# Plain second layer in the first two later groups, with the weights' sums made two groups later

## The chip, the cores and the metric

The kernel runs on one core of one Trainium2 chip. The time is that of the device in microseconds (us); 676.91 us is the median of three runs of the kernel before. A profile of one execution, 673.3 us long, gives the busy times and waits of the engines: TensorE (PE in the profile, its weight loads PEld), VectorE (DVE), ScalarE (ACT), GpSimd (POOL) and the DMA queues, of which SyncE (SP) issues nearly all.

## The reference

A recurrent attention block (a decaying state per head) feeds a two-layer block with a gate. All inputs are float32.

```python
# attention, for each time t, batch b, head h (4 batches, 8 heads, 768 steps, 64 wide)
state = gamma * state + outer(k[t], v[t])
y[t] = scale * q[t] @ state
x = y as (3072 tokens, 512)

# two-layer block: w_in (512, 2048), w_out (2048, 512)
h = x @ w_in
g = h * erf(softplus(h))
out = g @ w_out
```

## The kernel before

**Groups.** The 2048 hidden features are split, and so are the tokens. Groups 0 to 3 are the first 512 tokens with 512 features each, computed plainly. From group G0 = 4 up to 23 come the later groups, to which the change belongs: 256 tokens (a "chunk") and 1024 features each, so two groups, `s = 0` and `s = 1`, make a chunk, and both add into the same outputs. Group 4 and 5 are the first chunk of these, 6 and 7 the second.

**First layer of a later group.** `hidden_steps` (L951) computes 26 products of sums in place of 32 plain ones: 26 steps of two matmuls 128x128x128. A float32 matmul leaves two records in the trace, so a step is four records. Each step's product goes to one of four PSUM tiles (banks 0 and 1 are called `hp`, 2 and 3 `r`), and is added to or subtracted from blocks of `h`: the first write of a block is a copy on ScalarE (L974, L976), each later one an addition on VectorE (L972). A step that writes a tile waits for the reads of what was in it. Step 5 is the first with an update on VectorE; steps 1, 5, 9, 13, 15, 16, 19 and 23 to 25 use bank 0. The weights of the steps are sums of blocks of `w_in`, made in place once (`W_SUMS`, `sum_in`, L344): those of `s = 0` on VectorE during group 4, of `s = 1` twenty on GpSimd and ten on VectorE.

**The gate.** `gate_softplus` and `gate_erf` run on ScalarE over 128x2048 values, and `gated` (L854) multiplies on VectorE; the result is `E[g]`, in the buffer `e` (or `r` for groups 1 and 3).

**Second layer of a later group.** `project_part` (L1015) makes seven products of four matmuls with 256 columns (eight records), in place of eight in a plain one: `PRODUCTS` pairs sums of gated values (`S1` to `S4`, made by `g_sums`, L1009, four additions) with sums of weights (`T1` to `T4`). The latter are made once for each `s` by `sums` (L354), each an operation of 128x1024 on VectorE; `last_steps` hands them out one by one. `put_part` (L1041) adds the products up into outputs on VectorE. The plain second layer of groups 0 to 3 is `project` (L890), with 512 columns, whose matmuls are at L901, and `put_first` copies out.

**The order** is written by hand. The loop over `g` issues group g's steps; between steps `order` says after which step n a piece of other work is issued: the next chunk's scalings and transposes (`prepared`: L542, L551 twice, L555 twice), `g_sums`, `last_steps`. After steps 14, 18 and 24 comes a product of group g - 1, and after the loop the attention of a later chunk (`sub_visit`, L718) and group g - 1's other products. Each engine works its own queue in the order of issue, so an operation on VectorE holds up all that is issued behind it.

The sums of `w_out` for `s = 0` are issued at the end of group 4 (two) and after steps 1 and 3 of group 5 (two, ahead of step 5's update). Those for `s = 1` are issued after step 22 of group 5, after steps 12 and 22 of group 6, and at the end of group 6. The last plain steps of group 3, `project(3, 0)` and `project(3, 1)`, stand ahead of group 4's loop, the two others behind it:

```python
    project(G0 - 1, 0)
    x_sums(G0)
    sub_begin(j)
    project(G0 - 1, 1)
    sub_states(j)
    sum_in(0, 20)
```

`x_sums` (L942) makes the sums of inputs on VectorE. `sub_begin` makes scores into two tiles `r` on TensorE, and `sub_states` reads these on VectorE (L640, L666).

Of the kernel before, what the change touches and what calls it, by code (L numbers as in the profile page):

```python
# [12 lines left out]
F32 = mybir.dt.float32  # L13
# [6 lines left out]
P = 128  # L20
C = 128
TCH = 512
FG = 4
SCH = 256
# [112 lines left out]
def kernel(  # L137
# [13 lines left out]
    nc = tc.nc  # L151
# [10 lines left out]
    DH = d_model // 2  # L162
# [555 lines left out]
    def sub_visit(j, g):  # L718

        c = j % NC
        m, i = divmod(j, JPC)
        if i == 0:
            XC[m] = ret.tile([P, HP, TCH], F32, name="xT")
        pp = [ret_psum() for _ in range(2)]
        clear = set()

        def first(*bank):  # L730
            new = bank not in clear
            clear.add(bank)
            return new

        def of_state(a):
            t = slice(a * D, (a + 1) * D)
            for u in PAIRS:
                for r in range(2):
                    col, own = u // 2, slice(r * D, (r + 1) * D)
                    x = state_1 if g == G0 else state  # L740
                    nc.tensor.matmul(  # L741
                        pp[r][col * D : (col + 1) * D, u % 2, t], x[own, u, :], QT[j][own, u, t],
                        start=first(r, col), stop=True, skip_group_check=True,
                    )

        other = SC[j + 1] = [ret_psum(ps_h) for _ in range(2)]

        def of_values(crossed):  # L750
            for u in PAIRS:
                for a in range(2):
                    r = 1 - a if crossed else a
                    col, t = u // 2, slice(a * D, (a + 1) * D)
                    own = slice(col * D, (col + 1) * D)
                    nc.tensor.matmul(
                        other[a][own, u % 2, D:] if crossed else pp[a][own, u % 2, t],
                        V[j][t, 2 * u + r, :],
                        AM[j][t, r, u, :D],
                        start=crossed or first(r, col), stop=True, skip_group_check=True,  # L760
                    )

        if c:
            of_state(0)
        last = chunk_of(g - 1)
        if (g - G0) % 2 == 1:
            clear.update((("o", 0), ("o", 1)))
        new = [
            None if g == G0 else O[last][3][:, 1, :].rearrange("p (u d) -> p u d", d=D),
            pp[1][:, 2:, :].rearrange("p a (b d) -> p (a b) d", d=D),  # L770
        ]
        adds = range(int(g == G0), 2 if c < NC - 1 else 1)
        for u in range(HP):
            for r in range(2):
                for a in adds:
                    t, h = slice(a * D, (a + 1) * D), 2 * u + r
                    nc.tensor.matmul(  # L777
                        new[a][r * D : (r + 1) * D, u, :], KQ[j][t, 0, h, :], V[j][t, h, :],
                        start=first("o" if a == 0 else 1, r), stop=True, skip_group_check=True,
                    )  # L780
        if g > G0 and c:
            nc.vector.tensor_tensor(state, state, new[0], op=ALU.add)
        elif g > G0:
            nc.vector.tensor_copy(state, new[0])
        of_values(False)
        of_values(True)
        if j + 1 < NJ:
            sub_scores(j + 1)
            sub_mask(j + 1)
        of_state(1)  # L790
        for r in range(2):
            a = 1 - r
            x, y = XC[m][:, r::2, i * C : (i + 1) * C], other[a][:, :2, D:]
            if c or a:
                nc.scalar.copy(x, pp[r][:, :2, :])
                x = x[:, :, a * D : (a + 1) * D]
                nc.vector.tensor_tensor(x, x, y, op=ALU.add)
            else:
                nc.scalar.copy(x[:, :, D:], pp[r][:, :2, D:])
                nc.scalar.copy(x[:, :, :D], y)  # L800
        if c < NC - 1:
            nc.vector.tensor_tensor(state, state_1 if g == G0 else state, new[1], op=ALU.add)
# [14 lines left out]
    def gate_softplus(g):  # L817


        name = "r" if g < 4 and g % 2 else "e"  # L820
        E[g] = act.tile([P, N], F32, name=name, bufs=1)
        nc.scalar.activation(E[g], HS[g], AF.Softplus)  # L822

# [97 lines left out]
    G0 = n_ft // FG  # L921
# [5 lines left out]
    def chunk_of(g):  # L927
        return TCH // SCH + (g - G0) // 2
# [109 lines left out]
    started = set()  # L1038
    R = {}

    def put_part(m, step):  # L1041


        o26, o57, o34, o1 = (O[m][i] for i in range(4))
        if step == 0:
            R[m] = act.tile([P, 8, DH], F32, name="r", bufs=1)
            nc.scalar.copy(R[m][:, 7], o1[:, 0])
            return
        r = R[m]
        t0 = m * SCH  # L1050
        if step == 1:
            nc.vector.tensor_tensor(
                r[:, 0:5:4], o26, r[:, 7:8].to_broadcast([P, 2, DH]), op=ALU.add
            )
        elif step == 2:
            nc.vector.tensor_tensor(
                r[:, 5:7], o57, r[:, 4:5].to_broadcast([P, 2, DH]), op=ALU.add
            )
            nc.vector.tensor_tensor(r[:, 3], r[:, 6], o57[:, 0], op=ALU.add)
        else:  # L1060
            nc.vector.tensor_tensor(r[:, 1:3], r[:, 5:7], o34, op=ALU.add)
            for t in range(2):
                nc.sync.dma_start(
                    out[t0 + t * P : t0 + (t + 1) * P, :],
                    r[:, 2 * t : 2 * t + 2].rearrange("p a c -> p (a c)"),
                )
# [103 lines left out]
    def all_of(steps):  # L1170
        for _ in steps:
            pass
# [10 lines left out]
    project(G0 - 1, 0)  # L1183
    x_sums(G0)
    sub_begin(j)
    project(G0 - 1, 1)
    sub_states(j)
    sum_in(0, 20)

    put = None  # L1190
    for g in range(G0, NG):
        first, even = g == G0, (g - G0) % 2 == 0
        more = j < NJ
        if put is not None:
            put_part(put, 0)
        e_sums = iter(()) if first else g_sums(g - 1)
        next(e_sums, None)
        next_chunk = prepared(j + 1) if even or put is None else iter(())

        if put is not None:  # L1200
            order = {18: (e_sums,), 20: (e_sums,), 24: (e_sums, e_sums)}
        else:
            order = {
                10: (next_chunk,), 14: (next_chunk, e_sums), 16: (next_chunk, e_sums),
                18: (next_chunk, e_sums), 20: (e_sums,), 24: (next_chunk,),
            }
        if g == G0 + 1:
            order.update({1: (last_steps,), 3: (last_steps,), 22: (last_steps,)})
        elif g == G0 + 2:
            order.update({12: (last_steps,), 22: (last_steps,)})  # L1210
        for n, _ in enumerate(hidden_steps(g), start=1):
            if first:
                sum_in(0, min(20 + n, len(W_SUMS)))
                if n == 10:
                    nc.gpsimd.tensor_copy(idle[:, :1], w_in_sb[:, 0, W_SUMS[-1][0], :1])
                    sum_in(1, 20, nc.gpsimd)
            if put is not None and n in (14, 16, 18):
                put_part(put, n // 2 - 6)
            for steps in order.get(n, ()):
                next(steps, None)  # L1220
            if not first and n in (14, 18, 24):
                project_part(g - 1, {14: 1, 18: 2, 24: 4}[n])
        put = None
        all_of(e_sums)
        all_of(next_chunk)

        nc.scalar.activation(idle[:, 1:], idle[:, 1:], AF.Softplus)
        gate_softplus(g)
        if more:
            sub_visit(j, g)  # L1230
        if g + 1 < NG and not even:
            x_sums(g + 1)
        if more:
            if even and not first:
                all_of(prepared(j + 2))
            if j + 3 < NJ:
                load(j + 3)
            j += 1
        gate_erf(g)
        if first:  # L1240
            sum_in(1, len(W_SUMS))
            for tt in range(2, TT):
                project(g - 1, tt)
            put_first()
        else:
            if g == G0 + 2:
                all_of(last_steps)
            for p in (5, 6, 7, 3):
                project_part(g - 1, p)
            if even:  # L1250
                put = chunk_of(g - 1)
        if g == NG - 1:
            last_gated(g)
        else:
            gated(g)
        if first:
            for _ in range(2):
                next(last_steps)

    g, m = NG - 1, chunk_of(NG - 1)  # L1260
    for p, step in ((1, 0), (7, None), (2, None), (6, 1), (5, 2)):
# [56 lines left out]
```

## Time and profile before

| | us |
|---|---|
| time, median of 3 runs (lowest to highest) | 676.91 (675.51 to 677.26) |
| span of the profiled execution | 673.3 |
| TensorE busy | 657.0 |
| weight loads busy | 558.1 |
| VectorE busy | 519.7 |
| ScalarE busy | 272.1 |
| GpSimd busy | 23.0 |

A row of the order of time has the start and the length in us, the engine, the line, the operation, the tile written, the tiles read, shapes and the number of instructions merged into it; a bracket is the time that the engine idled before it, with what ended that. A list of waits has a total, the number of waits and the longest. A row of the windows has for each engine the busy time and the number of instructions, then the granted TensorE clock (1.00 is full), the share of the DMA engines and GB/s. Busy shares are a mean over stages: VectorE is busy 77% of the span, but in the stretch from 160 to 170 us it is busy 9.46 of 10 us and TensorE 5.42.

### The profile page before, as it was taken

What the parts mean: (1) busy time and instruction counts of PE and PEld (TensorE: products, weight loads), DVE (VectorE), ACT (ScalarE), POOL (GpSimd) and SP (SyncE); (2) the same over time, 40 slices, a digit from 0 to 9 for tenths busy, and PEclk for the clock granted to TensorE, in tenths of its full rate; (3) what the DMA queues carried; (4) which work ended last, traced back from release to release, by engine and by line L of the source; (5) the groups of instructions that cost most, each with busy time, mean ns of one, the idle gap of its engine ahead of it and who ended that gap; (6) DMA issues with size and microseconds to landing.
All of it is one profiled execution on the core that took longest, in us unless ns stands there. A gap on an engine that the chain in (4) does not pass through costs nothing.

```text
span 673.3 us, 15344 instructions
## 1 busy us (share of the span) xinstructions
PE 657.0 (98%) x6240; PEld 558.1 (83%) x6240; DVE 519.7 (77%) x1107; ACT 272.1 (40%) x394; POOL 23.0 (3%) x42
## 2 busy tenths in 40 slices
PE   8999999987998999999999999999999999999998
PEld 7744444474997999999999999999999999999997
DVE  5999999988888678677777787787688688476464
ACT  3467453325244243343442442542542542433440
POOL 1000000254000000000000000000000000000000
PEclk9999999999899999999999999999999999999999
DMA  9999953333222222232221231232232220000000
GB/s 187 227 246 217 223 146 87 62 62 59 88 45 45 69 37 46 34 80 45 43 70 33 46 79 35 46 77 38 43 78 40 39 59 1 1 34 1 1 32 32
DMA packets 156726, 47.70 MB, mean 71 GB/s; under 512 B 143088, under 2 KB 147568, under 8 KB 156656
## 3 DMA queue, kind: packets, MB, share of 16 engines
q1 hardware_dynamic: 156240, 46.72, 32.2%
q8 instruction: 49, 0.80, 0.5%
q14 instruction: 21, 0.17, 0.1%
q10 hardware_dynamic: 416, 0.01, 0.0%
HBM read 40.39 MB, written 6.29 MB: 69 GB/s over the span
## 4 chain that ended last, share of the span: by engine, by line
PE 90%; DVE 5%; SPq 2%; DMA 1%; issue 1%; ACT 1%; DVEq 0%; ACTq 0%
PE o L1027 35%; PE hp L960 21%; PE r L960 11%; PE hp L865 8%; PE o L901 7%; SPq L187 2%; PE r L741 1%; PE hp L633 1%; DVE w_in_sb L344 1%; PE o L777 1%; DVE h L972 1%; DVE w_out_sb L354 1%; DMA kq<-in_k_dram 1%; PE r L562 1%; PE o L609 1%
## 5 line engine op out<-in xcount | busy, mean ns | idle before, releaser
L960 PE MATMUL hp<-xs,w_in_sb 128*128 128x128 f32 x1040 | 147.0, 277 | 7.0 <-DVE h L972 6.1
L1027 PE MATMUL o<-w_out_sb,h 128*128 128x256 f32 (+1 forms) x648 | 144.1, 379 | 2.5 <-DVE w_out_sb L354 2.2
L960 PEld LDWEIGHTS hp<-xs,w_in_sb 128*128 128x128 f32 x1040 | 135.7, 193 | 11.3 <-DVE h L972 7.4
L972 DVE TENSOR_TENSOR h<-h,hp 128x256 f32<-128x256 f32 x200 | 81.9, 418 | 75.0 <-PE hp L960 70.2
L1027 PEld LDWEIGHTS o<-w_out_sb,h 128*128 128x128 f32 x648 | 120.5, 190 | 19.6 <-DVE w_out_sb L354 2.6
L1027 PE MATMUL o<-w_out_sb,e 128*128 128x256 f32 x480 | 114.1, 381 | 1.2 <-DVE w_out_sb L354 1.2
L1027 PEld LDWEIGHTS o<-w_out_sb,e 128*128 128x128 f32 x480 | 87.3, 191 | 11.0 <-DVE w_out_sb L354 1.4
L822 ACT ACTIVATE e<-h 128x2048 f32<-128x2048 f32 x22 | 42.0, 1911 | 130.1 <-DVE h L972 130.0
L974 ACT COPY h<-hp 128x256 f32<-128x256 f32 x40 | 14.9, 373 | 154.1 <-PE hp L960 146.0
L972 DVE TENSOR_TENSOR h<-h,r 128x256 f32<-128x256 f32 x160 | 59.9, 415 | 21.6 <-PE r L960 20.5
L960 PE MATMUL r<-xs,w_in_sb 128*128 128x128 f32 x480 | 67.1, 276 | 0.0
L960 PEld LDWEIGHTS r<-xs,w_in_sb 128*128 128x128 f32 x480 | 60.3, 193 | 0.0
L865 PE MATMUL hp<-xT,w_in_sb 128*128 128x512 f32 (+2 forms) x144 | 56.5, 548 | 0.0
L854 DVE TENSOR_TENSOR e<-h,e 128x1024 f32<-128x1024 f32 x42 | 49.3, 1214 | 8.0 <-ACT e L835 8.0
L960 PE MATMUL hp<-xT,w_in_sb 128*128 128x128 f32 x320 | 48.7, 275 | 0.0
L865 PEld LDWEIGHTS hp<-xT,w_in_sb 128*128 128x128 f32 x144 | 25.8, 190 | 27.0 <-issue 24.6
L960 PEld LDWEIGHTS hp<-xT,w_in_sb 128*128 128x128 f32 x320 | 43.7, 192 | 1.9 <-issue 1.0
L835 ACT ACTIVATE e<-e 128x2048 f32<-128x2048 f32 (+1 forms) x23 | 42.1, 1836 | 0.2
L976 ACT ACTIVATE h<-hp 128x256 f32<-128x256 f32 x60 | 23.0, 384 | 35.3 <-PE hp L960 33.9
L960 PE MATMUL r<-xT,w_in_sb 128*128 128x128 f32 x240 | 33.3, 275 | 0.0
L835 ACT ACT_TABLE_LOAD x24 | 30.8, 1283 | 0.4
L960 PEld LDWEIGHTS r<-xT,w_in_sb 128*128 128x128 f32 x240 | 30.0, 192 | 0.0
(156 smaller groups left out, 774.9 us busy)
## 6 DMA issues: line engine op xcount, KB each, us to landing
w_out_sb<-in_moe_w_out_dram SPq DMA_DIRECT2D x14, 512.0 KB, 5.8
kq<-in_k_dram SPq DMA_DIRECT2D x23, 256.0 KB, 4.0
v<-in_v_dram SPq DMA_DIRECT2D x23, 256.0 KB, 3.2
out_dram<-r SPq DMA_DIRECT2D x23, 256.0 KB, 2.7
kq<-in_q_dram SPq DMA_DIRECT2D x288, 16.0 KB, 1.8
kb<-in_k_dram SPq DMA_DIRECT2D x288, 16.0 KB, 1.7
w_in_sb<-in_moe_w_in_dram SPq DMA_DIRECT2D x8, 512.0 KB, 12.1
w_in_sb<-in_moe_w_in_dram SPq DMA_DIRECT2D x8, 256.0 KB, 8.1
```

Source lines behind the costliest of these rows:

```text
L187: nc.sync.dma_start(to[part, u * C : (u + 1) * C].rearrange("p (a d) -> p a d", d=32), src[2 * u + s, :, d * 32 : (d + 1) * 32].rearrange( ...
L344: (engine or nc.vector).tensor_tensor(w_in_sb[:, s, to], w_in_sb[:, s, a], w_in_sb[:, s, b], op=OP[sign])
L822: nc.scalar.activation(E[g], HS[g], AF.Softplus)
L835: nc.scalar.activation(E[g][:, half], E[g][:, half], AF.Erf)
L854: nc.vector.tensor_tensor(E[g][:, half], HS[g][:, half], E[g][:, half], op=ALU.mult)
L865: nc.tensor.matmul(HP_[ft][:, t], w_in_of(ft, kk), XC[0][:, kk, t], start=(kk == 0), stop=(kk == n_k - 1),)
L901: nc.tensor.matmul(O[0][tt].rearrange("p (d c) -> p d c", d=2), E[g][:, u * TCH + tt * P : u * TCH + (tt + 1) * P], w_out_of(ft), start=(f ...
L960: nc.tensor.matmul(to[:, u, :], w_in_sb[:, s, w, u * P : (u + 1) * P], XS[m](x), start=first and u == 0, stop=True, skip_group_check=True,)
L972: nc.vector.tensor_tensor(h, h, of, op=ALU.add if plus else ALU.subtract)
L974: nc.scalar.copy(h, of)
L976: nc.scalar.activation(h, of, AF.Copy, scale=-1.0)
L1027: nc.tensor.matmul(O[m][i][:, half, at], G[g][a][:, u * P : (u + 1) * P], w_out_sb[:, s, OUT[b], u, at], start=i not in started, stop=(s = ...
```

## The change

Groups 4 and 5 compute the second layer plainly (`project_plain`): eight parts, each two matmuls with 512 columns, straight from the gated values and the loaded weights. So no sums are needed for them, and the weights' sums are issued later: `s = 0` in group 6 (after steps 12, 15, 20, 22), `s = 1` in group 7 (14, 16) and group 8 (12, 22). Their outputs are copied on ScalarE (`put_plain`) in group 7. Parts 3 to 7 read `E[g]` after the next gate has begun, so group 5's gate gets the buffer `r`. The attention's addition for the state in group 5, which had used half of a bank begun by a product, now begins its bank itself. Beside this, `project(3, 1)` is issued after step 10 of group 4 in place of ahead of its loop, and the pieces of `prepared` in group 4 come after steps 12, 16, 18, 20 and 22, where they came after 10, 14, 16, 18 and 24.

```diff
-        if (g - G0) % 2 == 1:
+        if (g - G0) % 2 == 1 and g > G0 + 1:
             clear.update((("o", 0), ("o", 1)))
...
-        name = "r" if g < 4 and g % 2 else "e"
+        name = "r" if g < G0 + 2 and g % 2 else "e"
...
+    def project_plain(g, i):
+        m, s = chunk_of(g), (g - G0) % 2
+        t, fh, pair = i // 4, i % 4 // 2, i % 2
+        if m not in O:
+            O[m] = {i: ps_o.tile([P, 2, DH], F32, name=f"o{i}") for i in (0, 1, 3)}
+        for u in range(2 * pair, 2 * pair + 2):
+            at = (2 * fh + t) * TCH + u * P
+            nc.tensor.matmul(
+                O[m][t],
+                E[g][:, at : at + P],
+                w_out_sb[:, s, 2 * fh : 2 * fh + 2, u, :],
+                start=(s == 0 and i % 4 == 0 and u == 0),
+                stop=(s == 1 and i % 4 == 3 and u == 3),
+                skip_group_check=True,
+            )
+
+    def put_plain(m, t):
+        if t == 0:
+            R[m] = act.tile([P, 8, DH], F32, name="r", bufs=1)
+        r = R[m][:, 2 * t : 2 * t + 2].rearrange("p a c -> p (a c)")
+        nc.scalar.copy(r, O[m][t].rearrange("p a c -> p (a c)"))
+        nc.sync.dma_start(out[m * SCH + t * P : m * SCH + (t + 1) * P, :], r)
...
     sub_begin(j)
-    project(G0 - 1, 1)
     sub_states(j)
...
-    put = None
+    plain, put = (G0, G0 + 1), None
...
-        if put is not None:
+        if put is not None and put > chunk_of(G0):
             put_part(put, 0)
-        e_sums = iter(()) if first else g_sums(g - 1)
+        e_sums = iter(()) if g - 1 in plain or first else g_sums(g - 1)
...
-        if g == G0 + 1:
-            order.update({1: (last_steps,), 3: (last_steps,), 22: (last_steps,)})
+        if first:
+            order = {n: (next_chunk,) for n in (12, 16, 18, 20, 22)}
         elif g == G0 + 2:
-            order.update({12: (last_steps,), 22: (last_steps,)})
+            order.update({n: (last_steps,) for n in (12, 15, 20, 22)})
+        elif g == G0 + 3:
+            order.update({n: (last_steps,) for n in (14, 16)})
+        elif g == G0 + 4:
+            order.update({n: (last_steps,) for n in (12, 22)})
...
                 if n == 10:
+                    project(g - 1, 1)
...
             if put is not None and n in (14, 16, 18):
-                put_part(put, n // 2 - 6)
+                if put > chunk_of(G0):
+                    put_part(put, n // 2 - 6)
+                elif n < 18:
+                    put_plain(put, n // 2 - 7)
...
-                project_part(g - 1, {14: 1, 18: 2, 24: 4}[n])
+                part = (14, 18, 24).index(n)
+                if g - 1 in plain:
+                    project_plain(g - 1, part)
+                else:
+                    project_part(g - 1, (1, 2, 4)[part])
...
-            if g == G0 + 2:
-                all_of(last_steps)
-            for p in (5, 6, 7, 3):
-                project_part(g - 1, p)
+            if g - 1 in plain:
+                for part in range(3, 8):
+                    project_plain(g - 1, part)
+            else:
+                for p in (5, 6, 7, 3):
+                    project_part(g - 1, p)
...
-        if first:
-            for _ in range(2):
-                next(last_steps)
```

## The prediction

> **What bounds the kernel now.** I read the page first, then TensorE's waits, then its order of time around each wait, then the clock in short windows, then VectorE's order of time beside it. On the page:
>
> ```profile
> PE 657.0 (98%) x6240; PEld 558.1 (83%) x6240; DVE 519.7 (77%) x1107; ACT 272.1 (40%) x394; POOL 23.0 (3%) x42
> PE   8999999987998999999999999999999999999998
> PEclk9999999999899999999999999999999999999999
> PE 90%; DVE 5%; SPq 2%; DMA 1%; issue 1%; ACT 1%; DVEq 0%; ACTq 0%
> ```
>
> TensorE is busy 98% of the span and carries 90% of the chain that ended last. What can be won without less arithmetic are its 16 us of idling, and the sliced row puts most of them in slices 9, 10 and 13 (one slice is 16.8 us), where the later groups begin. The list of waits, TensorE only, names what it waits for:
>
> ```profile
> PE hp L960 <- DVE h L972: 6.1, 3, 3.9
> PE o L1027 <- DVE w_out_sb L354: 3.4, 2, 2.2
> PE hp L960 <- ACT h L974: 0.7, 1, 0.7
> ```
>
> The order of time on TensorE puts them in groups: the first two lines are group 4 (the first later one), the next four are group 5, the last two are group 6. The bracket is the idle time ahead of the row.
>
> ```profile
> 143.81 0.71 PE L960 MATMUL hp<-xs,w_in_sb 128*128 128x128 f32 x4 [1.74 <-DVE h L972]
> 149.40 0.71 PE L960 MATMUL hp<-xs,w_in_sb 128*128 128x128 f32 x4 [0.51 <-DVE h L972]
> ...
> 161.91 0.68 PE L960 MATMUL hp<-xs,w_in_sb 128*128 128x128 f32 x4 [0.73 <-ACT h L974]
> ...
> 167.79 1.16 PE L960 MATMUL hp<-xs,w_in_sb 128*128 128x128 f32 x8 [3.85 <-DVE h L972]
> 168.78 1.47 PE L960 MATMUL r<-xs,w_in_sb 128*128 128x128 f32 x8
> 170.04 1.91 PE L960 MATMUL hp<-xs,w_in_sb 128*128 128x128 f32 x8
> ...
> 207.77 1.99 PE L1027 MATMUL o<-w_out_sb,e 128*128 128x256 f32 x8 [1.20 <-DVE w_out_sb L354]
> ...
> 218.48 3.72 PE L1027 MATMUL o<-w_out_sb,h 128*128 128x256 f32 x16 [2.15 <-DVE w_out_sb L354]
> ```
>
> After the wait of 3.85 us the same eight records take 1.47 and 1.91 us, where they take 1.06 elsewhere. The windows show why: the granted clock (the column after POOL) is halved.
>
> ```profile
> 168.00:170.00 2.00, 2.00 (x16) 2.00 (x16) 1.52 (x5) 0.39 (x1) 0.00 (x0) 0.82 0.21 33
> 170.00:172.00 2.00, 2.00 (x11) 2.00 (x10) 1.43 (x5) 0.00 (x0) 0.00 (x0) 0.50 0.15 25
> ```
>
> VectorE's order of time says what TensorE waited for: four sums of second-layer weights stand ahead of the updates of h in group 5. In group 4 eight sums of first-layer weights stand ahead of the first update.
>
> ```profile
> 133.78 0.41 DVE L666 COPY state<-r 128x256 f32<-128x256 f32 x1
> 134.11 3.13 DVE L344 TENSOR_TENSOR w_in_sb<-w_in_sb 128x256 f32<-128x256 f32 x8
> 138.16 0.42 DVE L972 TENSOR_TENSOR h<-h,hp 128x256 f32<-128x256 f32 x1 [0.92 <-PE hp L960]
> ...
> 162.53 4.87 DVE L354 TENSOR_TENSOR w_out_sb<-w_out_sb 128x1024 f32<-128x1024 f32 x4
> ```
>
> An undisturbed group is 25.92 us long (222.20 to 248.12 to 274.04 in the chain of waits). Group 5 runs from 159.24 to 191.88, 32.64 us; group 6 to 222.04, 30.16 us. They are 6.72 and 4.24 us too long: this is what the change is aimed at.
>
> [...] 3.85 us of idling was followed by the clock of 0.50, while 1.74 and 2.15 us left it at 1.00. [...] a first-layer sum takes 0.39 us (3.13 for eight) before GpSimd's twenty sums begin at 142.11, and 0.65 us (6.55 for ten, from 153.79) beside them.
>
> **The change, part by part.**
>
> *Second layer plain in groups 4 and 5.* Removed per group: 7 products of 8 records at 0.216 us (eight take 1.73 us in the chain), 12.1 us. Added: 8 parts of 4 records over 512 columns; sixteen such records (L901) take 6.97 us from 152.27 to 159.24, 0.436 each, so 32 take 13.9 us. All of it is on TensorE's path: +1.8 us for each group, +3.7 in all. The three parts inside the loop take 4 x 0.436 = 1.74 us each, as a product does; the excess falls after the loop, five parts for four products. VectorE loses eight sums of gated values (L1009, about 0.6 us each), which it had room for.
>
> *Weight sums taken out of groups 4 to 6.* Group 5 loses its 3.85 us and the slow clock behind it. The slow clock costs 1.9 us: the four pieces after the wait take 1.16, 1.30, 1.71 and 2.15 us in the chain, against 0.89 three times and 1.73. ScalarE's 0.73 us stays, since the copies of the first output still stand ahead of its copies of h. VectorE then reaches group 5's first update after the gating at about 163, when that update's matmuls are just done. Group 5 becomes 25.92 + 0.73 + 1.74 = 28.4 us, for 32.64: -4.2.
>
> *Group 6.* It loses the waits of 1.20 and 2.15 us for sums, since its parts read weights as loaded: 25.92 + 1.74 = 27.7. But four sums of 1.15 us now stand in VectorE's queue at steps 12, 15, 20 and 22. A first-layer step (two matmuls, four records, 0.447 us) writes a PSUM tile whose previous values VectorE must have added to h. Behind the sum at step 12 wait the two updates of steps 13 and 14; step 15 waits for them. Before has the same sum there, and its piece up to step 18 is 3.87 us long against 3.52 in group 7: 0.35. Behind the sum at step 22 and the one at 20 waits the update of step 24, for which step 25 waits: VectorE does them in 4.9 us, and TensorE is there 4.4 us after the part at step 18, so 0.4. Group 6 is 28.4, for 30.16: -1.7.
>
> *Groups 7 and 8.* In 7 two sums take the place of the 2.4 us of output additions (L1052 to L1061), and the output copies go to ScalarE, which idles 4 us there: nothing. In 8 a sum stands at step 12, as in group 6 of before: +0.4. The other, at step 22, is hidden behind the part at step 24.
>
> *Output and buffers.* Group 5's gate moves to the buffer "r", whose last store was issued at about 161, twenty us before: nothing. The state's addition starts its own bank: the same matmuls.
>
> *The plain step inside group 4.* This is the part with a price. The step (8 records, 3.5 us) leaves its place ahead of group 4's loop and stands after step 10. TensorE so begins the loop at 132.2 for 135.8, while VectorE, the slower of the two there, begins its eight sums at 134.11 as before. I carried the rows' durations along both queues. Step 3 needs a tile that L666 reads until 134.19: TensorE waits 1.2 us. Step 9 needs the tile that step 5's update reads; that update is behind the eight sums and ends at 137.65: another 0.8. Steps 9 and 10 end at 138.6 and the moved step at 142.1. VectorE has ended its sums at 140.6 and idles 2.2 us, until step 11 gives it something. From there it is late: four updates, the scaling of keys (0.6 us, 0.9 beside GpSimd) and then step 13's update, for which step 15 waits 1.6 us; step 23 waits 0.4; and step 25 waits 1.7 us for an update that stands behind both transposes, since the second now comes at step 22 and not 24. That sums to 5.7 us of waits and ends the loop at 152.9. The same walk along the old queues gives 3.0 us of waits and 150.3, and the trace has 2.6 and 150.4. So +2.6 us. No single wait reaches the 3.85 us that halved the clock, so I put nothing for it.
>
> *Sum.* +2.6 - 4.2 - 1.7 + 0.4 = -2.9 us, which I take as -3.0; 676.91 becomes 673.9.
>
> **The rivals.**
>
> *A: the moved step fills waits, as it is meant to.* The 1.74 us wait is just where it is put, and if VectorE is not late, group 4 costs nothing: -2.9 - 2.6 = -5.5, 671.4. Against it: VectorE idles only 1.4 us in group 4 before.
>
> *B: the gain is half eaten.* The close waits of group 4 (1.2 and 0.8 us within 5 us) lower the clock as at 168, +1.9: -1.0, 675.9. [...] Against it: 2.6 us of work lie between them.
>
> *C: slower.* In before, three sums cost group 6 most of 4.2 us. If the eight sums in groups 6 to 8 (9.7 us) still hold up TensorE for half their length, 4.9 for the 1.2 us I put (0.75 and 0.4), the sum is -3.0 + 3.7 = +0.7, and with B's clock +2.6: 679.5. Against it: no matmul waits for these sums themselves any more.
>
> **How the numbers follow.** The forecast gets 0.5, A 0.22, B 0.18, C 0.10. The bound of 0.3% is 2.0 us: faster is below 674.9. The forecast is there in 17 cases of 20, A always; B is within, C slower or within. Faster 0.64, same 0.26, slower 0.10. The range, 670.8 to 677.2, reaches past A by the 0.6 us that the two waits put into group 6 and 8 could fall short, and up to B with 1.3 us more, leaving C's worse end out.
>
> **What would show it.** Right: no wait for L354 is left in TensorE's list; group 5 has no wait over 1 us and a clock of 1.00; groups 5 and 6 are about 28.4 us long; group 4's loop shows waits before steps 3, 9, 15 and 25 and ends about 2.6 us later, with VectorE idle near 141 to 143. Wrong: a clock under 1.00 in group 4, or waits over 1 us in groups 6 to 8 for L972.

## The result and the profile after

The changed kernel takes 672.50 us (median of four runs, 672.36 to 672.79) for 676.80 (675.51 to 677.26): a ratio of 0.994, 95% interval 0.9923 to 0.9957. The whole interval lies below the prediction's bound of 0.3% (0.997), so the change is faster. The forecast was 673.9. The profiled executions, 675.38 us before and 672.36 after, have spans of 673.3 and 670.3 us: 3.0 us apart, which is what the forecast took off.

The page of the changed kernel, busy times and slices:

```profile
PE 658.7 (98%) x6192; PEld 547.4 (82%) x6192; DVE 510.6 (76%) x1095; ACT 272.8 (41%) x395; POOL 22.1 (3%) x42
PE   8999999989999999999999999999999999999998
PEclk9999999999999999999999999999999999999999
```

TensorE is busy 1.7 us longer in a span that is 3.0 us shorter. The dents in slices 10 and 13 and the one in the clock are gone; slice 9 keeps one. TensorE's list of waits:

```profile
PE hp L960 <- DVE h L972: 3.8, 5, 1.4
...
PE r L960 <- DVE am L640: 0.8, 1, 0.8
PE hp L960 <- ACT h L974: 0.7, 1, 0.7
```

No wait for L354, a sum of second-layer weights, is left. The longest wait for an update of h is 1.4 us where it was 3.9. There are more of them, and TensorE's order of time says where:

```profile
133.94 1.13 PE L960 MATMUL r<-xs,w_in_sb 128*128 128x128 f32 x8 [0.75 <-DVE am L640]
...
137.57 1.16 PE L960 MATMUL hp<-xs,w_in_sb 128*128 128x128 f32 x8 [0.71 <-DVE h L972]
138.56 3.60 PE L901 MATMUL o<-w_out_sb,r 128*128 128x512 f32 x8
...
145.22 0.71 PE L960 MATMUL hp<-xs,w_in_sb 128*128 128x128 f32 x4 [1.27 <-DVE h L972]
...
149.23 1.16 PE L960 MATMUL hp<-xs,w_in_sb 128*128 128x128 f32 x8 [0.18 <-DVE h L972]
151.75 0.71 PE L960 MATMUL hp<-xs,w_in_sb 128*128 128x128 f32 x4 [1.36 <-DVE h L972]
...
164.26 0.68 PE L960 MATMUL hp<-xs,w_in_sb 128*128 128x128 f32 x4 [0.73 <-ACT h L974]
...
206.78 0.71 PE L960 MATMUL hp<-xs,w_in_sb 128*128 128x128 f32 x4 [0.27 <-DVE h L972]
```

The rows from 133.94 to 151.75 are group 4: TensorE waits before steps 3, 9, 15, 23 and 25, with the moved plain step (L901) at 138.56 between. VectorE's order of time in the same stretch shows the other side:

```profile
139.56 0.87 DVE L344 TENSOR_TENSOR w_in_sb<-w_in_sb 128x256 f32<-128x256 f32 x2
142.72 1.42 DVE L972 TENSOR_TENSOR h<-h,r 128x256 f32<-128x256 f32 x4 [2.28 <-PE r L960]
144.05 0.78 DVE L542 TENSOR_TENSOR kq<-kq,kq_s 128x512 f32<-128x512 f32 x1
```

VectorE, the slower engine of this group, idles 2.28 us while TensorE does the moved step. In the stretch of group 5 where the clock fell before, it now stays at 1.00:

```profile
165.00:170.00 5.00, 5.00 (x39) 4.37 (x38) 3.79 (x10) 1.14 (x3) 0.00 (x0) 1.00 0.24 39
170.00:175.00 5.00, 5.00 (x31) 3.72 (x30) 3.15 (x7) 1.86 (x3) 0.00 (x0) 1.00 0.66 208
```

Read from the starts of the groups on TensorE:

| stretch | before, us | forecast | changed, us |
|---|---|---|---|
| group 5 begins at | 159.24 | +2.6 | 161.58 (+2.3) |
| group 5 | 32.64 | 28.4 | 28.53 |
| group 6 | 30.16 | 28.4 | 28.47 |
| group 7 | 25.92 | 25.9 | 25.92 |
| group 8 | 25.92 | 26.3 | 26.35 |

Summed, the last column against the first is +2.34 - 4.11 - 1.69 + 0.43 = -3.03 us. So what the trace shows is accounted for. Left are the 1.3 us between this and the medians' 4.3, and the question whether each price was rightly understood: the move inside group 4, the plain layer, the clock.

### The profile page after: what moved, and what is told of

Read it like the earlier page. It is cut to its first block, busy times and chain, and to the rows that moved or that the text cites. A ratio compares the mean times of both kernels' runs of the same rounds, so it can differ in the third digit from the quotient of the medians.

```text
span 670.3 us, 15241 instructions
## 1 busy us (share of the span) xinstructions
PE 658.7 (98%) x6192; PEld 547.4 (82%) x6192; DVE 510.6 (76%) x1095; ACT 272.8 (41%) x395; POOL 22.1 (3%) x42
## 4 chain that ended last, share of the span: by engine, by line
PE 77%; DVE 9%; SPq 5%; issue 3%; DMA 3%; ACT 2%; DVEq 0%; ACTq 0%
PE o L1027 33%; PE hp L960 22%; PE r L960 11%; SPq L187 4%; PE o L1048 4%; DMA kq<-in_k_dram 2%; PE r L741 2%; PE hp L633 1%; DVE w_out_sb L317 1%; PE o L901 1%; DVE w_out_sb L325 1%; PE o L777 1%; DVE xs L325 1%; DVE h L972 1%; DVE w_in_sb L331 1%
## 5 line engine op out<-in xcount | busy, mean ns | idle before, releaser
L1027 PE MATMUL o<-w_out_sb,h 128*128 128x256 f32 (+1 forms) x584 | 129.5, 379 | 0.4 <-DVE r L1306 0.4
L1027 PEld LDWEIGHTS o<-w_out_sb,h 128*128 128x128 f32 x584 | 108.6, 190 | 15.4 <-DVE r L1306 0.6
L1027 PE MATMUL o<-w_out_sb,e 128*128 128x256 f32 x432 | 102.2, 379 | 0.0
L822 ACT ACTIVATE e<-h 128x2048 f32<-128x2048 f32 x21 | 40.1, 1911 | 123.0 <-DVE h L972 123.0
L1027 PEld LDWEIGHTS o<-w_out_sb,e 128*128 128x128 f32 x432 | 78.2, 191 | 8.5
L854 DVE TENSOR_TENSOR e<-h,e 128x1024 f32<-128x1024 f32 x40 | 46.9, 1214 | 8.1 <-ACT e L835 8.1
L835 ACT ACTIVATE e<-e 128x2048 f32<-128x2048 f32 (+1 forms) x22 | 40.2, 1833 | 0.2
```

What stands on the lines that cost most here:

```text
L835: nc.scalar.activation(E[g][:, half], E[g][:, half], AF.Erf)
L854: nc.vector.tensor_tensor(E[g][:, half], HS[g][:, half], E[g][:, half], op=ALU.mult)
L1027: nc.tensor.matmul(O[m][i][:, half, at], G[g][a][:, u * P : (u + 1) * P], w_out_sb[:, s, OUT[b], u, at], start=i not in started, stop=(s = ...
```

## The experiments

Theory: a sum or a step costs what it delays in VectorE's queue, and a wait of TensorE like the 3.85 us of before costs a second time through the clock (1.9 us there by the prediction's estimate). Rivals: the plain step in group 4 is a help or neutral; prices simply add; only the plain layer can make room for the sums. The kernel before ran beside them, with medians of 676.98, 676.97 and 676.45 us in the three sets of runs. Its runs at one and the same mean clock, 0.997, have medians of 675.66, 675.44 and 675.48 us, so times of different sets can be laid side by side to within some 0.2 us.

**Group 4's edits undone, in the changed kernel.**

```diff
     sub_begin(j)
+    project(G0 - 1, 1)
     sub_states(j)
...
-            order = {n: (next_chunk,) for n in (12, 16, 18, 20, 22)}
+            order = {n: (next_chunk,) for n in (10, 14, 16, 18, 24)}
...
-                    project(g - 1, 1)
```

> The changed kernel with both edits inside group 4 undone (the plain step of group 3 ahead of the loop again, the pieces of the next chunk after steps 10, 14, 16, 18, 24). Theory of the two queues (VectorE is the slower engine in group 4, so starting TensorE's steps earlier only makes it wait, and the moved step then lets VectorE idle): TensorE's waits in group 4 fall from 4.3 to about 2.6 us, group 5 begins at about 159.2 us in place of 161.6, and nothing after it changes: span 668.0, time 2.3 us under the changed kernel, 670.2. Rival (the plain step fills waits that would be there anyway): the waits of step 15 return beside nothing gained, and the time is 672.5 or more.

Measured: 670.39 us (670.02 to 671.96), ratio 0.9905 (0.9885 to 0.9924), span 668.0. The rows of group 4 are those of before:

```profile
143.82 0.71 PE L960 MATMUL hp<-xs,w_in_sb 128*128 128x128 f32 x4 [1.74 <-DVE h L972]
149.41 0.71 PE L960 MATMUL hp<-xs,w_in_sb 128*128 128x128 f32 x4 [0.51 <-DVE h L972]
```

The edits inside group 4 cost the change 672.50 - 670.39 = 2.1 us of its gain, 2.3 us between the profiled spans.

**One of the two at a time.** First only the step put back ahead of the loop (first and last hunk above), then only the order of the pieces (the middle hunk).

> The changed kernel with only the plain step of group 3 put back ahead of group 4's loop; the pieces of the next chunk stay after steps 12, 16, 18, 20, 22. Theory of the two queues: waits before step 15 (2.0 us), 23 (0.4) and 25 (1.7) remain, the loop ends 1.0 to 1.4 us earlier than in the changed kernel: 671.3. If the place of the step alone were the price, all 2.3 us would come back: 670.2. If the order of the pieces alone were the price, nothing: 672.5.

> The changed kernel with only the pieces of the next chunk put back to steps 10, 14, 16, 18, 24 of group 4; the plain step stays after step 10. Theory of the two queues: the waits before steps 3 and 9 stay (1.5 us together), those before 15 and 25 fall to 0.7 each; the loop ends 1.6 to 1.8 us earlier: 670.8. If the place of the step alone were the price: 672.5.

Measured: 672.02 us (671.72 to 672.08) with the step back, 670.76 (670.60 to 670.88) with the order back. The second is as expected. The first is 0.7 us above its number: the step's place gives 0.5 us back, and the order of the pieces 1.7. With the order back, the waits before steps 15 and 25 are 0.56 and 0.51 us, for 1.27 and 1.36 in the changed kernel. In the run with the step back the clock fell in group 4:

```profile
142.00:146.00 4.00, 1.95 (x16) 1.76 (x15) 3.77 (x8) 0.45 (x2) 3.92 (x6) 0.95 0.23 36
146.00:150.00 4.00, 4.00 (x25) 4.00 (x25) 3.35 (x7) 1.41 (x2) 3.61 (x6) 0.62 0.21 33
```

The wait ahead of it was 2.05 us long. But the one run of five whose mean clock was 1.000 took 671.88 us, hardly less than the 672.03 of the four at 0.997. Here the slow clock seems to take the place of waits for VectorE: before steps 23 and 25 the list has 0.7 us, where 2.1 were expected. So the clock doesn't account for the 0.7 us of the miss; what does was not shown.

**Only group 4's edits, in the kernel before.**

```diff
-    project(G0 - 1, 1)
     sub_states(j)
...
-        if g == G0 + 1:
+        if first:
+            order = {n: (next_chunk,) for n in (12, 16, 18, 20, 22)}
+        elif g == G0 + 1:
...
                 if n == 10:
+                    project(g - 1, 1)
```

> The kernel before with only the two edits inside group 4 (plain step after step 10, pieces after 12, 16, 18, 20, 22); second layer and weight sums as before. Theory of slack: group 4 ends 2.3 us later as in the changed kernel, but VectorE, which holds up group 5, isn't later, because its ten first-layer sums run beside less of GpSimd's work; so group 5's wait falls from 3.9 to about 1.6 us and the clock isn't halved: net +2.3 - 2.3 - 1.9 = -1.9 us, about 675 for 676.8. Rival (the parts add up): +2.3 us, 679.

Measured: 675.84 us (674.08 to 677.77), ratio 0.9979 (0.9970 to 0.9989). The same edits that cost 2.1 us in the changed kernel gain 1.1 here; the prices don't add. Group 5 begins at 161.89, and the longest waits of groups 5 and 6 are

```profile
168.30 1.16 PE L960 MATMUL hp<-xs,w_in_sb 128*128 128x128 f32 x8 [1.72 <-DVE h L972]
...
217.35 5.37 PE L1027 MATMUL o<-w_out_sb,h 128*128 128x256 f32 x16 [2.15 <-DVE w_out_sb L354]
```

1.72 us for 3.85: TensorE came 2.7 us later, VectorE only 0.5 (the wait for its first update of h in group 5 ends at 168.30 for 167.79). In the changed kernel, which has the same edits in group 4, its ten first-layer sums ahead of these updates take 4.40 us for 6.55 in before (GpSimd's own end at 156.53 for 158.40). This is the slack of the theory. The second row shows that group 6's wait of 2.15 us, harmless in the profile of before (3.72 us for the sixteen records after it), here was followed by 5.37 us, with the clock at 0.55 from 217 to 220. Eight of the 22 runs have a mean clock of 1.000 and take 674.08 to 674.42 us; the other 14, at 0.997, have a median of 675.91. The theory's 1.9 us were thus missed by 0.8 at the median, because in most runs the clock fell after all; the one profile, of a run at 0.997, has the fall at group 6's wait, and group 5's windows at 1.00.

**Three sums ahead of group 5's updates, for four**, in the kernel before.

```diff
-            order.update({1: (last_steps,), 3: (last_steps,), 22: (last_steps,)})
+            order.update({1: (last_steps,), 15: (last_steps,), 22: (last_steps,)})
```

> The kernel before with one of the four weight sums that stand ahead of group 5's first update (the fourth, T3 of s = 0) moved to after step 15 of group 5. Theory [...]: group 5's wait falls from 3.9 to about 2.6 us, the clock stays at 1.00, and the time falls by 1.2 + 1.9 = 3.1 us, to 673.7; the runs also spread less. Rival (the clock's loss shrinks with the wait, or isn't bound to it): 1.2 to 1.8 us, 675.3.

Measured: 675.73 us (674.42 to 677.39), 1.2 us less than before: the rival's number. The wait was 2.71 us and the clock fell all the same, for longer than in the profile of before:

```profile
166.00:169.00 3.00, 2.45 (x11) 2.45 (x12) 1.85 (x5) 0.34 (x1) 0.00 (x0) 0.50 0.24 39
169.00:172.00 3.00, 3.00 (x16) 3.00 (x15) 1.92 (x5) 0.05 (x1) 0.00 (x0) 0.50 0.16 26
172.00:175.00 3.00, 3.00 (x19) 2.67 (x18) 2.92 (x5) 0.00 (x0) 0.00 (x0) 0.89 0.84 255
```

That the clock stays at 1.00 after a wait shorter than the 3.85 us of before was an estimate of mine: that part of my theory fell.

**The sums spread, no plain layer**, in the kernel before.

```diff
-            order.update({1: (last_steps,), 3: (last_steps,), 22: (last_steps,)})
+            order.update({12: (last_steps,), 15: (last_steps,), 20: (last_steps, e_sums), 22: (last_steps,)})
         elif g == G0 + 2:
-            order.update({12: (last_steps,), 22: (last_steps,)})
+            order.update({12: (last_steps,), 15: (last_steps,), 20: (last_steps, e_sums), 22: (last_steps,)})
...
-        if first:
-            for _ in range(2):
-                next(last_steps)
```

> The kernel before, second layer by seven products everywhere, with its eight weight sums merely spread: four after steps 12, 15, 20 and 22 of group 5, four after the same steps of group 6, and none ahead of group 5's updates. Group 4 as before. If the deferral is what pays and the plain layer is only a way to it, group 5 is 25.9 + 0.7 + 2.8 = 29.4 us (32.6 before) and group 6 25.9 + 2.8 = 28.7 (30.2 before): span 668.7, time 671.4 or so, about 1 us better than the changed kernel. If VectorE can't carry four sums beside the sums of gated values, each group loses 4 us or more and the time is 674 or above.

Measured: 671.13 us (670.98 to 671.27), groups 5 and 6 29.8 and 28.6 us long. Spreading the sums alone beats the change by 1.4 us; against the changed kernel with group 4 undone it is 0.7 slower. Its groups 5 and 6 are 3.9 and 2.7 us longer than an undisturbed one, the changed kernel's 2.6 each: spread like this, the sums of groups 5 and 6 cost somewhat more than the plain layer with its sums in group 6 (and 0.4 us in group 8).

**The plain step after step 8**, in the changed kernel with the old order of pieces.

```diff
-            order = {n: (next_chunk,) for n in (12, 16, 18, 20, 22)}
+            order = {n: (next_chunk,) for n in (10, 14, 16, 18, 24)}
...
+                if n == 8:
+                    project(g - 1, 1)
                 if n == 10:
-                    project(g - 1, 1)
```

> The changed kernel with the plain step of group 3 after step 8 of group 4 in place of step 10, and the pieces of the next chunk after steps 10, 14, 16, 18, 24. Theory of the two queues: step 9 has to wait for step 5's update anyway, so the plain step fills that wait, the wait of step 3 stays, and the loop ends 0.4 us earlier than with the step ahead of the loop: 669.8, 2.7 us under the changed kernel. Rival (any place inside the loop costs): as with the step after step 10 and these pieces, 670.8.

Measured: 670.83 us (670.50 to 671.10), span 668.8, the rival's number. The step fills the wait before step 9, but the wait before step 3 remains (0.75 us) and that before step 15 is 1.33. My number had left the first out of the sum, though the text names it: -0.4 + 0.75 is near the +0.4 us measured against the step ahead of the loop (670.83 for 670.39). Neither of the two places inside the loop that were tried did better than the one ahead of it.

**Each sum where VectorE idles, no plain layer**, in the kernel with the sums spread.

```diff
         if g == G0 + 1:
-            order.update({12: (last_steps,), 15: (last_steps,), 20: (last_steps, e_sums), 22: (last_steps,)})
+            order.update({5: (last_steps,), 10: (last_steps, next_chunk), 19: (last_steps,), 24: (next_chunk, last_steps)})
         elif g == G0 + 2:
-            order.update({12: (last_steps,), 15: (last_steps,), 20: (last_steps, e_sums), 22: (last_steps,)})
+            order.update({1: (last_steps,), 5: (last_steps,), 14: (last_steps, next_chunk, e_sums), 24: (next_chunk, last_steps)})
```

> As the run with the sums spread over steps 12, 15, 20 and 22, second layer by seven products everywhere and group 4 as before, but each sum is put where VectorE idles anyway: after steps 5, 10, 19 and 24 of group 5 and after 1, 5, 14 and 24 of group 6. Theory (the waits come from what a sum delays behind it, not from VectorE lacking time): group 5 is 25.9 + 0.7 + 0.3 = 27.0 us, group 6 25.9; span 673.3 - 5.7 - 4.2 = 663.4, time 665.6, well under the changed kernel without any plain layer. Rival (VectorE lacks the time for four sums beside the sums of gated values): as the spread one, 671.1.

Measured: 666.42 us (666.29 to 666.65), ratio 0.9856 (0.9844 to 0.9869), span 664.2: the fastest of all, 6.1 us below the changed kernel. The only rows of TensorE in groups 5 and 6 that show a wait are these two:

```profile
161.83 0.68 PE L960 MATMUL hp<-xs,w_in_sb 128*128 128x128 f32 x4 [0.73 <-ACT h L974]
...
168.47 0.71 PE L960 MATMUL hp<-xs,w_in_sb 128*128 128x128 f32 x4 [0.21 <-DVE h L972]
```

VectorE had the time for all eight sums; only their places were wrong. In group 5 it now works with hardly a pause from 162.62 to 178.1 us, and still hardly keeps TensorE waiting. Group 5 is 27.8 us and group 6 26.0. What group 5 has over 25.92 + 0.73 lies ahead of step 15, where TensorE stands for 0.4 us (168.10 to 168.47), and in the attention after step 26: from that step's start to the next product TensorE takes 2.92 us (177.01 to 179.93), in group 6 2.56. The remaining 0.4 us I could not place.

**The same for the changed kernel**, with group 4's edits undone.

```diff
-            order.update({n: (last_steps,) for n in (12, 15, 20, 22)})
+            order.update({1: (last_steps,), 5: (last_steps,), 14: (last_steps, next_chunk), 24: (next_chunk, last_steps)})
...
-            order.update({n: (last_steps,) for n in (12, 22)})
+            order.update({n: (last_steps,) for n in (1, 5)})
```

> The changed kernel with group 4's edits undone and its sums put into VectorE's idle places too: after steps 1, 5, 14 and 24 of group 6, 14 and 16 of group 7, 1 and 5 of group 8. No wait for a displaced update should be left in groups 6 and 8: 0.7 us less than with group 4 undone alone, or 669.4 to 669.7. Beside the run with the same places and no plain layer it gives the plain layer's price alone: 3.7 us by the sum of records (two groups, 13.9 for 12.1 us each); if the plain layer also freed VectorE for something, less.

Measured: 668.91 us (668.71 to 668.97). The sums cost nothing any more in groups 6 and 8: group 8 is 25.92 us again, and group 6 is 215.64 - 188.08 = 27.56 us, so the plain layer costs 27.56 - 25.92 = 1.6 us there. Moving the sums gave 0.9 us in group 6 and 0.4 in group 8, where 0.7 in all was expected. Against the kernel with the same places and no plain layer, the plain layer loses 2.5 us in all; it isn't the full 3.3, since group 5 then holds no sums (28.5 us beside 27.8).

**Only one group's sums moved**, in the kernel before: those of s = 1, then those of s = 0.

```diff
-            order.update({1: (last_steps,), 3: (last_steps,), 22: (last_steps,)})
+            order.update({1: (last_steps,), 3: (last_steps,)})
         elif g == G0 + 2:
-            order.update({12: (last_steps,), 22: (last_steps,)})
+            order.update({1: (last_steps,), 5: (last_steps,), 14: (last_steps, next_chunk, e_sums), 24: (next_chunk, last_steps)})
```

> The kernel before with only the sums of s = 1 moved, into idle places of group 6 (after steps 1, 5, 14, 24); the four sums of s = 0 still stand ahead of group 5's updates. Group 6's 4.2 us of excess go, group 5's 6.7 stay: 4.2 us less in runs with the same clock, 671.3. If the second drop of the clock that most runs of before have comes from group 6's waits, it is gone as well, nearly all runs are at a mean clock of 0.997, and the median falls by 5.5 us to 671.4; if it comes from group 5's wait, the runs stay spread over 1.5 us or more with the median near 672.7.

```diff
-            order.update({1: (last_steps,), 3: (last_steps,), 22: (last_steps,)})
+            order.update({5: (last_steps,), 10: (last_steps, next_chunk), 19: (last_steps,), 22: (last_steps,), 24: (next_chunk, last_steps)})
...
-        if first:
-            for _ in range(2):
-                next(last_steps)
```

> The kernel before with only the sums of s = 0 moved, into idle places of group 5 (after steps 5, 10, 19, 22); those of s = 1 nearly as before (after 24 of group 5, 12 and 22 of group 6, and its end), so group 6 still waits 1.2 and 2.2 us. Group 5's waits of 3.9 and the clock behind them go, 5.7 us with the clock at 1.00: 669.7. If group 6's waits lower the clock by themselves in some runs, these are at 0.997 and 1.6 us longer, 671.3, and the times fall into two heaps.

Measured: 672.22 us (671.32 to 672.60) and 672.73 (671.66 to 673.65). With group 5's wait left, the expected 4.2 us came at the same clock (671.32 for 675.5 us at 0.997), but only one of five runs is at 0.997 and four are at 0.995: group 5's wait alone can bring the longer loss of clock. Its profile, of a run at 0.995, has the clock low over three windows:

```profile
165.00:168.00 3.00, 0.00 (x0) 0.00 (x0) 2.96 (x5) 0.00 (x0) 0.00 (x0) 0.74 0.22 36
168.00:171.00 3.00, 2.87 (x13) 2.87 (x14) 1.43 (x4) 0.38 (x1) 0.00 (x0) 0.50 0.26 40
171.00:174.00 3.00, 3.00 (x16) 2.93 (x15) 2.37 (x7) 0.00 (x0) 0.00 (x0) 0.62 0.77 232
```

With group 6's waits left, the times fall into two heaps, as expected, though both 2 us higher: 671.7 to 671.9 at a clock of 0.999 to 1.000, and 673.5 to 673.7 at 0.997. Group 5 is 28.9 us there, for 27.0 expected. It holds five sums, and the one after step 22 stands ahead of the update for which step 25 waits, a wait that the run with the sums after 5, 10, 19 and 24 doesn't have:

```profile
177.74 0.71 PE L960 MATMUL hp<-xs,w_in_sb 128*128 128x128 f32 x4 [0.94 <-DVE h L972]
```

## Why the prediction was right, and where it was off

*The bound* was right: TensorE, with VectorE's queue deciding its waits in groups 4 to 6.

*Group 5*: 28.4 forecast, 28.53 measured. The 3.85 us and the slow clock went, ScalarE's 0.73 us stayed, the plain layer's part was added. VectorE came to the group's first update with time to spare (it idles 2.24 us ahead of it, until 165.05), where the forecast had it just in time.

*Group 6*: 28.4 forecast, 28.47 measured. The wait before step 15 came as in before (a gap of 0.3 us that the list leaves out), that before step 25 was 0.27 us for 0.4.

*Groups 7 and 8*: nothing and +0.4 forecast; nothing and +0.43 measured.

*The plain step inside group 4*: +2.6 forecast, +2.3 in the trace, 2.1 by undoing it. The places of the waits were right (before steps 3, 9, 15, 23 and 25). The list has 4.3 us of them for the walk's 5.7, but it leaves short stops out: from the loop's start to the attention behind it (132.04 to 152.83, in before 135.66 to 150.49) TensorE takes 5.7 us more than the 26 steps of 0.447 us and the moved step of 3.4 us, in before 3.2. So the walk's sums, 5.7 and 3.0, came out nearly as walked. Undoing one at a time shows what the forecast didn't separate: 1.7 us belong to the order of the pieces, 0.5 to the step's place.

*The plain layer*: +1.8 us a group forecast, 1.6 measured in group 6, with its sums out of the way.

*Where it was off: the term for the slow clock, and the base.* The sum gave -3.0 us and the profiled runs are 3.0 us apart. But it was worked out from a profiled run of 675.38 us and taken off a median of 676.91; off its own run it gives 672.4, and 672.5 was measured. The profiled run was one of the mildest. Of the 54 runs of before in the first two sets, the 15 with a mean clock of 0.997 have a median of 675.5 us, the 27 at 0.995 of 677.0, the 7 at 0.994 of 677.3 and the 5 at 0.992 of 678.0. The change's four runs lie at 0.999 to 1.000. So the term for the slow clock was 1.9 us where the usual run loses about 1.9 + 1.5 = 3.4. The runs with one group's sums moved put most of the rest behind group 5's wait (four of five runs at 0.995 with group 6's waits gone) and some behind group 6's (three of six at 0.997 with group 5's gone), for which the prediction had no clock term. Where the clock fell in runs that were not profiled is inferred from this.

*The rivals.* A, the moved step fills waits: refuted by the run that undoes it. B, a clock lowered by the new waits of group 4: not in any of the change's runs (mean clocks 0.999 to 1.000), though with only the step back a wait of 2.05 us in group 4 was followed by 0.62 (146 to 150). C, slower: the list has no wait over 0.3 us in groups 6 to 8.

## What to carry to other kernels

What a late operation costs is what stands behind it in its engine's queue: the same eight sums cost about 10 us in one order, 6 in another and 1 in a third (groups 5 and 6 beside 25.92 us each, without ScalarE's 0.73; the 10 hold the slow clock), and adding arithmetic to avoid them was the dearer way. A step moved to fill the faster engine's wait can starve the slower one (VectorE idled 2.28 us for it), and a delay that is harmless ahead of another wait has its full price once that wait is gone (group 4's edits gained 1.1 us with it and cost 2.1 without). An estimate made from one profiled run is to be taken off that run's own time.

## What the runs showed of the hardware

A single wait of TensorE of 2.05 us (only the step back), 2.15 (only group 4's edits) or 2.71 (three sums ahead) came with a fall of the granted clock, to windows of 0.62, 0.55 and 0.50. The wait of 2.15 us was followed by the fall in the profile with only group 4's edits and not in those of before (1.00 from 205 to 228), of three sums ahead (1.00 from 205 to 250) and of only s = 0 moved (mean clock of the whole run 1.000). With 1.74 us as the longest wait of the loop over groups, none of 18 runs of four kernels (group 4 undone, the sums spread, and the two with sums where VectorE idles) had a mean clock under 0.999. How long a wait must be was not shown: 2.15 us did both.

The falls were of two lengths. Estimated from the windows (the missing share of clock, times the window's length, over 0.5) the clock was halved for 3.4 us in the profiles of before (0.36 + 1.00 + 0.34 = 1.70 us missing, the last from 172 to 174 at 0.83), of the run with only the step back (0.20 + 1.52), and of the run with only group 4's edits (1.35 + 0.36); and for 6.8 us in those with three sums ahead (0.09 + 1.50 + 1.50 + 0.33) and with only s = 1 moved (0.78 + 1.50 + 1.14).

Which of the two it was goes with the time of the fall in all five profiles. In the first three the clock fell 1.5 us after the wait had ended (169.3 for 167.79), 1.3 us after (145.6 for 144.34) and just at its end (217.3 for 217.35). In the other two it fell while TensorE still waited, 0.7 us ahead of the end (165.8 for 166.55) and 1.7 us ahead (166.4 for 168.13). My estimate is that the heaps of before, 1.5 us apart, are runs with the one length and with the other: 1.70 us missing from a span of 673.3 give a mean clock of 0.9975, twice that 0.995; the heaps are at 0.997 and 0.995. What decides between them was not shown.
